# Writing one sum into another row, and tracing one block's routing later, in a fused attention, gated FFN and mixture-of-experts kernel

## The chip, the cores and the metric

One core of a Trainium2 chip runs the whole program. The metric is the device time of one execution in microseconds (us); lower is better.

## The reference, cut to what matters

```python
attn_out = _attn_ref(q, k, v)             # 4 x 8 heads x 576 positions x 64, window 128
x = attn_out -> [2304, 512]
gate = 1 / (1 + exp(-(x @ w_gate)));  val = x @ w_val          # 512 -> 1536
x = (gate * val) @ w_out                                        # 1536 -> 512
logits = xn @ en.T / tau; expert_idx = argmax(logits)           # 8 experts, one per token
out[mask] = gate_w * (relu(x[mask] @ w1[e]) @ w2[e])            # 512 -> 1024 -> 512
```

Everything is float32 to the outside. The kernel splits each matmul operand into a high and a low part and adds three products.

## The kernel before, in words

**Attention** comes first, then **the gated FFN's first matrix pair** (`w_gate`, `w_val`) in two passes over the 12 feature tiles f, each pass on two token chunks of 512. Both passes use a scheme of seven products instead of eight (`seven`): per f the products m5, m6, m7, m4 and m3 of f and m1 and m2 of f+1 alternate on TensorE (PE), six matmuls of 128x512 each. Their sums are collected on ScalarE (ACT; copies `c11`, `r1`, `c22`, the tanh `c21`) and VectorE (DVE). Line 438 is the matmul in `product`; L527, L532, L535, L538 and L542 are the ACT steps e1, e2, e6, e7 and e4; L531, L539 and L549 are the DVE additions.

In the second pass the gated values are not stored plainly. `keep_g` computes (gate+1)*val (L458), for each pair kk of feature tiles f = 2kk and 2kk+1 and both token halves, and stores through `put` (L461, a DMA issued by GpSimd, POOL) the four quarters A11, A12, A21, A22 and four sums S1 to S4 of them (L464 on DVE), because **the second matrix `w_out`** is applied to these 1024 tokens by a seven-product scheme again. In the even tile the values go to the halves `low` and `high` of a tile `gq`; in the odd tile they go to the gate's own row. The odd tile's second call (half 0) computes A12 into the gate's row (tile `c11`, in the profile `c`), issues its store, and then computes S4 = A12 - S2 into that same row and stores it. S4 occurs six times, once for each odd f. Rows are 128x512 tiles from a pool of ten.

While f runs, ACT and DVE also convert one tile of `w_out` (`split_wo`: L125 on ACT, L131, L132 and L134 on DVE into `cvwo`, then the cast `wo<-cvwo` at L105 on ACT and the subtraction at L121 on DVE), and POOL stores `cvwo`.

**The second matrix**: blocks of 256 tokens. Blocks 4, 3, 2, 1, 0 (`ROWS`) are done plainly (`mm2`, L914, 12 k-tiles in order); ahead of block 2 stands the scheme `strassen` for the 1024 tokens kept in the second pass (blocks 5 to 8): seven operands j, each two halves z (`mm3(j, z)`, L1228, 18 matmuls), with `ev3` scaling the results. The operand of j+1 is cast and subtracted at the head of step j (`split_op`, `oh` on ACT and `ol` on DVE). `prepare(0)` also builds four differences of `w_out` for each of six pairs (`split_w2`: `tq`, `th`, `tl`).

**Routing of a block**: `route_x` scales the two result banks into rows `xr` (L927) and squares them back into the banks (L928). `route_a` transposes `xr` (L954), copies to `xT` (DVE, L955), multiplies by the expert embeddings (`part`, L961), copies `parts` (ACT, L965), folds (`lp`, L969), normalises, takes the maximum and the exponentials, and stores the rows (two DMAs on POOL, L990). `route_b` counts ranks (`rk`, L1007 to L1012) and scatters token numbers (two indirect DMAs on POOL, L1030). Block 4 is routed during block 3's `mm2`; block 3 (`ROWS[1]`) is routed inside `strassen`: before the change in step j = 0.

PSUM banks: tag `m` has three, `s` two, `t` two, `o` one. The two banks of a block's `mm2`, the `a` accumulators and the `c` accumulator of half 0 share `m`; `part`, `lp` and the `c` accumulator of half 1 (first used in `mm3(1, 1)`) share `s`.

**What sets the order.** In the attention blocks and the first pass the order is written by hand. From the second pass on, a planner of the framework sets each engine's order at compile time, with its own estimate of durations; among instructions that are ready by the estimate, the one traced earlier goes first. On the chip each engine then runs its own list in that order, and waits where an estimate was off.

Of the kernel before, what the change touches and what calls it, by code (L numbers as in the profile page):

```python
# [15 lines left out]
ALU = mybir.AluOpType  # L16
# [25 lines left out]
ROWS = [4, 3, 2, 1, 0]  # L42
# [18 lines left out]
def attn_ffn_moe(ctx: ExitStack, tc: tile.TileContext, qkd, vd, wgv, w_out, emb, tau, w1, w2, cst, ids, out):  # L61
# [19 lines left out]
    def pt(tag, name, bufs):  # L81
        return ps.tile([P, 512], F32, tag=tag, name=name, bufs=bufs)

    def row(name):
        return mid.tile([P, DM + 16], F32, tag="r", name=name)[:, 0:DM + 1]

    def slot(shape, dt, name):
        return bpool.tile(shape, dt, tag="b", name=name)
# [359 lines left out]
    def g7_rows(name, kk, n=1):  # L448
        r = (NAMES.index(name) * KF // 2 + kk) * P
        return g7_d[r:r + n * P, :]  # L450

    def keep_g(f, half, gate, val):
        kk, odd = divmod(f, 2)
        if not odd and kk not in gq:
            gq[kk] = slot([P, 2, 512], F32, f"gq{kk}")
        low, high = gq[kk][:, 0, :], gq[kk][:, 1, :]
        o = gate if odd else (low, high)[half]
        nc.vector.scalar_tensor_tensor(out=o, in0=gate, scalar=1.0, in1=val, op0=ALU.add, op1=ALU.mult)  # L458

        def put(name, t):  # L460
            nc.gpsimd.dma_start(g7_rows(name, kk), t)  # L461

        def sums(name, t, x, y, op):
            nc.vector.tensor_tensor(out=t, in0=x, in1=y, op=op)  # L464
            put(name, t)

        if odd or not half:
            put(f"A{half + 1}{odd + 1}", o)
        if not odd and not half:
            sums("S3", high, high, low, ALU.subtract)  # L470
        elif odd and half:
            sums("S2", high, o, high, ALU.add)
            sums("S1", low, high, low, ALU.add)
        elif odd:
            sums("S4", o, o, high, ALU.subtract)

    def piece(mm, ev):
        def both():
# [243 lines left out]
    with tc.manual_schedule(engines={ENG.PE, ENG.DVE, ENG.Activation, ENG.Pool}):  # L722
        for i in range(NA, NU):
# [5 lines left out]
            late = unit_b(i)  # L729
# [87 lines left out]
    for f in range(KF):  # L817
        s, t = sv[f], sv[f + 1] if f + 1 < KF else None
# [127 lines left out]
    def route_a(b, ss, xr, c=None):  # L946
        nu = len(xr)
        lg = sm.tile([P, nu, E], F32, tag="lg", name=f"lg{b}")
        if c is None:
            xT = slot([P, nu, DM], F32, f"xT{b}")  # L950
        for u, x in enumerate(xr if c is None else []):
            q = pt("t", f"tl{b}_{u}", 2)
            for k in range(KD):
                nc.tensor.transpose(q[:, k * P:(k + 1) * P], x[:, k * P:(k + 1) * P], ident)  # L954
            nc.vector.tensor_copy(xT[:, u, :], q)  # L955
        part = pt("s", f"part{b}", 2)
        w = P // KD
        t0 = (2 * b * P - 256) % 512
        for k in range(KD):
            o = part[k * w:(k + 1) * w, 0:nu * P]  # L960
            nc.tensor.matmul(o.rearrange("p (u t) -> p u t", u=nu) if c is None else o, enT[:, k, :],  # L961
                             xT[:, :, k * P:(k + 1) * P] if c is None else c[k // 2][:, k % 2, t0:t0 + 2 * P],
                             start=True, stop=True, tile_position=(0, k * w))
        parts = row(f"parts{b}")[:, 0:nu * P]
        nc.scalar.copy(parts, part[:, 0:nu * P])  # L965
        lp = pt("s", f"lp{b}", 2)
        lps = [lp[:, u * E:(u + 1) * E] for u in range(nu)]
        for u in range(nu):
            nc.tensor.matmul(lps[u], parts[:, u * P:(u + 1) * P], fold, start=(u == 0), stop=(u == nu - 1),  # L969
                             skip_group_check=True)  # L970
        rn = rnorm(ss, nu, f"x{b}")
        mx = sm.tile([P, nu, 8], F32, tag="mx8", name=f"mx8{b}")
        ix = sm.tile([P, nu, 8], U32, tag="ix8", name=f"ix8{b}")
        nmx = sm.tile([P, nu], F32, tag="nmx", name=f"nmx{b}")
        sx = sm.tile([P, nu], F32, tag="sx", name=f"sx{b}")
        ex = sm.tile([P, nu, E], F32, tag="ex", name=f"ex{b}")
        for u in range(nu):
            nc.vector.tensor_scalar(out=lg[:, u, :], in0=lps[u], scalar1=rn[:, u:u + 1], scalar2=itau,
                                    op0=ALU.mult, op1=ALU.mult)
            nc.vector.max(out=mx[:, u, :], in_=lg[:, u, :])  # L980
            nc.vector.max_index(out=ix[:, u, :], in_max=mx[:, u, :], in_values=lg[:, u, :])
        nc.vector.tensor_scalar_mul(nmx, mx[:, :, 0], -1.0)
        for u in range(nu):
            nc.scalar.activation(out=ex[:, u, :], in_=lg[:, u, :], func=AF.Exp, bias=nmx[:, u:u + 1],
                                 accum_out=sx[:, u:u + 1])
        nc.vector.tensor_scalar_add(sx, sx, 1e-9)
        for u in range(nu):
            nc.vector.reciprocal(out=xr[u][:, DM:DM + 1], in_=sx[:, u:u + 1])
            t0 = (2 * b + u) * P
            (nc.sync if b == ROWS[-1] else nc.gpsimd).dma_start(x2_d[t0:t0 + P, :], xr[u])  # L990
        ixf = sm.tile([P, nu], F32, tag="ixf", name=f"ixf{b}")
        nc.vector.tensor_copy(ixf, ix[:, :, 0])
        oh = sm.tile([P, nu, E], BF16, tag="oh", name=f"oh{b}")
        for u in range(nu):
            nc.vector.tensor_scalar(out=oh[:, u, :], in0=iota8, scalar1=ixf[:, u:u + 1], scalar2=None,
                                    op0=ALU.is_equal)
        routed[b] = (oh, ixf)
# [221 lines left out]
    def mm3(j, z, k0=0, k1=KF // 2):  # L1219
        name, w, b = STEPS2[j]  # L1220
        first = j in (0, 1, 6)
        if first and k0 == 0:
            bk[b, z] = pt("s" if (b, z) == ("c", 1) else "m", f"{b}{z}_2", 2 if (b, z) == ("c", 1) else 3)
        for kk in range(k0, k1):
            wh, wl = w2_of(w, kk, z)
            xl, xh = (t[:, kk % 2, :] for t in g7[j][kk // 2])
            for y, (p, q) in enumerate(((wh, xh), (wl, xh), (wh, xl))):
                nc.tensor.matmul(bk[b, z], p, q, start=(first and kk == 0 and y == 0), stop=(kk == KF // 2 - 1 and y == 2),  # L1228
                                 skip_group_check=True)

    def ev3(j, z):
        def half(key, b):
            if key not in cq:
                cq[key] = slot([P, 2, 512], F32, f"c{key}")
            nc.scalar.mul(cq[key][:, z, :], bk[b, z], 0.5)

        def add(key, b):
            o = cq[key][:, z, :]
            nc.vector.scalar_tensor_tensor(out=o, in0=bk[b, z], scalar=0.5, in1=o, op0=ALU.mult, op1=ALU.add)

        if j == 0:
            half("11", "a")
        elif j == 2:
            half("12", "a")
        elif j == 3:
            half("22", "a")
            add("22", "c")
        elif j == 4:
            half("21", "a")
        elif j == 5:  # L1250
            add("12", "c")
        elif j == 6:
            add("11", "b")

    def strassen(late):
        xs2 = {}

        def rx(b):
            xs2[b] = route_xs(b, [cq["21"], cq["22"]] if b < 7 else [cq["11"], cq["12"]])

        def ra(b):
            route_a(b, *xs2.pop(b))

        load_op(2)
        mm3(0, 0, 0, 2)
        route_a(ROWS[1], *late)
        mm3(0, 0, 2)
        ev3(0, 0)
        mm3(0, 1, 0, 3)
        route_b(ROWS[1])  # L1270
        mm3(0, 1, 3)
        ev3(0, 1)
        for j in range(1, 7):
            split_op(j + 1)
            load_op(j + 2)
            if j == 5:
                load_g(ROWS[2])
            for z in range(2):
                mm3(j, z, 0, 3)
                for t in {(5, 0): [lambda: rx(5)], (5, 1): [lambda: ra(5)], (6, 0): [lambda: ra(6), lambda: route_b(5)],  # L1280
                          (6, 1): [lambda: route_b(6)]}.get((j, z), []):
                    t()
                mm3(j, z, 3)
                ev3(j, z)
                if (j, z) == (5, 1):
                    rx(6)
        split_g(ROWS[2])
        load_g(ROWS[3])
        return {0: [lambda: rx(7)], 1: [lambda: rx(8), lambda: ra(7)], 2: [lambda: route_b(7), lambda: ra(8)],
                3: [lambda: route_b(8)]}  # L1290
# [13 lines left out]
    for i, b in enumerate(ROWS):  # L1304
        inner = {}
        if i == STRASSEN_AT:
            inner = strassen(late)
# [29 lines left out]
        late = route_x(b, m)  # L1337
# [218 lines left out]
```

## Time and profile before

| what | value |
|---|---|
| time, median of 2 runs | 842.18 us (841.26 and 843.11) |
| the profiled execution | 838.87 us, span 837.1 us |
| PE busy | 796.3 us, 95% of the span |
| DVE busy | 567.8 us, 68% |
| ACT busy | 449.0 us, 54% |
| POOL busy | 208.2 us, 25% |
| mean granted TensorE clock | 0.98 |

The profile is of one execution. Times of rows are in us from the span's start. "Busy" is the time in which at least one instruction of the engine ran; "idle before" is the wait of an engine before an instruction, with what released it. A row of the time line reads: start, duration, engine, line, operation, out<-in, form, count, and in brackets the idle time before it. The second pass of `seven` runs from about 270 to 395 us, `mm2` of blocks 4 and 3 from 396 to 438 us, step j = 0 of the scheme from 438 to 458 us, steps j = 1 and 2 until about 476 us.

### The profile page before, as it was taken

Reading aid. Unit: us, or ns where it says so; the run is one execution under the profiler, and the core shown is the slowest. Engines: PE = TensorE matmul, PEld = TensorE weight load, DVE = VectorE, ACT = ScalarE, POOL = GpSimd, SP = SyncE. Lnnn points to the kernel's source line nnn. Section 1 sums busy time; section 2 is a strip of 40 time slices with the busy share of each in tenths; the row PEclk is TensorE's granted clock in tenths of the full one; section 3 lists DMA queues with packets and bytes.
Section 4 is the critical chain, followed back from the end, with each engine's and each line's share of the span. In section 5 each row is a group of like instructions: output and inputs, shape, how many; then the busy total and the mean of one; then the engine's idle time right before and its main releaser. Section 6 shows DMA issues by size and latency. Waiting matters only on the chain. (4 is left out here: it accounts for less than half of the span.)

```text
span 837.1 us, 15636 instructions
## 1 busy us (share of the span) xinstructions
PE 796.3 (95%) x5562; PEld 659.4 (79%) x5563; DVE 567.8 (68%) x1430; ACT 449.0 (54%) x946; POOL 208.2 (25%) x330
## 2 busy tenths in 40 slices
PE   8989999999999999896897999998999999999997
PEld 6767878878888887775685888776989989889796
DVE  7988977787799777766577666754846464455621
ACT  6888766666555544454446567744335443344510
POOL 6757422222000122222201203331231220310300
PEclk9999999999999999999797999999999999999999
DMA  8686567645754899878734684241568545545200
GB/s 276 190 272 213 193 240 226 244 168 214 245 221 154 327 332 323 297 270 301 246 106 142 182 278 175 102 141 49 165 183 330 182 160 188 179 152 177 80 23 17
DMA packets 71070, 166.61 MB, mean 199 GB/s; under 512 B 9511, under 2 KB 23591, under 8 KB 70992
## 3 DMA queue, kind: packets, MB, share of 16 engines
q1 hardware_dynamic: 61136, 136.08, 48.1%
q0 software_dynamic: 9856, 29.53, 9.8%
q8 instruction: 44, 0.72, 0.3%
q14 instruction: 34, 0.28, 0.1%
HBM read 116.20 MB, written 50.03 MB: 199 GB/s over the span
## 5 line engine op out<-in xcount | busy, mean ns | idle before, releaser
L1116 PE MATMUL h<-xe,weh 128*128 128x256 f32 (+4 forms) x512 | 107.7, 304 | 0.0
L1134 PE MATMUL z<-weh,h 128*128 128x512 f32 (+3 forms) x320 | 101.5, 396 | 0.9 <-DVE h L1119 0.6
L117 POOL TENSOR_SCALAR p<-p,rs 128x192 f32<-128x192 f32 x140 | 76.0, 560 | 102.1 <-DVE rs L268 51.7
L1116 PEld LDWEIGHTS h<-xe,weh 128*128 128x128 f32 x512 | 85.9, 194 | 1.2 <-DVE h L1119 0.2
L121 DVE TENSOR_TENSOR wel<-wer,weh 128x1024 fp32r<-128x1024 f32 x64 | 77.1, 1221 | 14.1 <-ACT weh L105 6.6
L914 PE MATMUL y<-wo,gh 128*128 128x512 f32 x240 | 80.0, 407 | 1.4 <-ACT gh L105 1.4
L1116 PE MATMUL h<-xe,wel 128*128 128x256 f32 (+4 forms) x256 | 77.7, 304 | 0.0
L252 ACT ACTIVATE p<-p,mx 128x192 f32<-128x192 f32 x144 | 64.0, 447 | 24.3 <-DVE mx L249 24.0
L105 ACT CAST weh<-wer 128x1024 fp32r<-128x1024 f32 x64 | 66.4, 1048 | 11.7 <-PE z L1134 9.7
L1118 ACT ACTIVATE h<-h 128x256 fp32r<-128x256 f32 (+4 forms) x64 | 26.7, 418 | 81.3 <-PE h L1116 76.5
L1134 PEld LDWEIGHTS z<-weh,h 128*128 128x128 f32 (+3 forms) x320 | 56.6, 181 | 15.6 <-DVE h L1119 1.0
L1139 POOL DMA_INDIRECT out<-y,cols x19 | 22.2, 1170 | 169.7 <-DVE y L1138 159.1
L1134 PE MATMUL z<-wel,h 128*128 128x512 f32 (+3 forms) x160 | 62.7, 392 | 0.0
L1119 DVE SCALAR_TENSOR_TENSOR h<-h,h 128x256 fp32r<-128x256 f32 (+4 forms) x64 | 29.5, 464 | 47.1 <-ACT h L1118 46.8
L914 PEld LDWEIGHTS y<-wo,gh 128*128 128x128 f32 x240 | 46.1, 194 | 12.5 <-ACT gh L105 1.8
L914 PE MATMUL y<-wo,gl 128*128 128x512 f32 x120 | 48.3, 403 | 4.6 <-DVE gl L121 4.6
L1138 DVE TENSOR_SCALAR y<-z,xg 128x512 f32<-128x512 f32 (+3 forms) x22 | 16.4, 747 | 49.3 <-PE z L1134 45.6
L1116 PEld LDWEIGHTS h<-xe,wel 128*128 128x128 f32 x256 | 49.7, 194 | 0.0
L461 POOL DMA_DIRECT2D g_d<-gq x24 | 13.3, 554 | 98.2 <-DVE gq L458 89.1
L249 DVE CUSTOM_DVE_ANT_0 p<-s,bias 128x192 f32<-128x192 f32 x96 | 30.7, 350 | 8.4 <-PE s L238 8.4
L238 PE MATMUL s<-qk 64*64 64x128 f32 (+2 forms) x864 | 34.2, 276 | 1.6 <-DVE mx L249 0.7
L281 PE MATMUL t<-cs,p 128*128 128x128 f32 x216 | 31.7, 279 | 3.9 <-ACT xf L105 2.5
(469 smaller groups left out, 2111.8 us busy)
## 6 DMA issues: line engine op xcount, KB each, us to landing
wer<-in_w SPq DMA_DIRECT2D x64, 512.0 KB, 7.1
wr<-in_wgv SPq DMA_DIRECT2D x24, 512.0 KB, 4.9
qk<-in_qkd SPq DMA_DIRECT2D x36, 320.0 KB, 5.1
ol<-g_d SPq DMA_DIRECT2D x21, 512.0 KB, 7.1
gl<-gT_d SPq DMA_DIRECT2D x15, 512.0 KB, 4.0
v<-in_vd SPq DMA_DIRECT2D x36, 192.0 KB, 3.4
wor<-in_w_out SPq DMA_DIRECT2D x12, 512.0 KB, 5.0
g_d<-gq POOLq DMA_DIRECT2D x24, 256.0 KB, 4.9
```

Of the source, the lines that this page charges most:

```text
L105: nc.scalar.copy(o, i)
L117: nc.gpsimd.tensor_scalar(out=t, in0=t, scalar1=r, scalar2=0.0, op0=ALU.mult, op1=ALU.add)
L121: e.tensor_tensor(out=o, in0=i, in1=h.bitcast(F32), op=ALU.subtract)
L238: nc.tensor.matmul(ss[u][y * 64:(y + 1) * 64, j * WK + d:j * WK + d + n], q[halves[u], a:a + 64], k[halves[u], a + c0:a + c0 + n], start=T ...
L249: nc.vector.tensor_tensor_reduce(out=o, in0=ss[u][:, j * WK:(j + 1) * WK], in1=bias, scale=-0.125, scalar=3.0e38, op0=ALU.add, op1=ALU.min ...
L252: nc.scalar.activation(out=o, in_=o, func=AF.Exp, scale=-1.0, bias=mx[:, z:z + 1], accum_out=su[:, z:z + 1])
L281: nc.tensor.transpose(t[:, z * P:(z + 1) * P], pf[:, z * P:(z + 1) * P], ident)
L914: nc.tensor.matmul(m, g[:, k % 4, u * P:(u + 1) * P], w[:, k % 3, :], start=(k == 0 and z == 0), stop=(k == KF - 1 and z == 2))
L1116: nc.tensor.matmul(m[:, :n], w[:, fs], x[:, k, :], start=(cnt == 0), stop=(cnt == 3 * KD - 1))
L1118: nc.scalar.activation(out=hh, in_=m[:, :n], func=AF.Relu)
L1119: nc.vector.scalar_tensor_tensor(out=hl, in0=m[:, :n], scalar=0.0, in1=hh.bitcast(F32), op0=ALU.max, op1=ALU.subtract)
L1134: nc.tensor.matmul(m[0:w, :], h, ww[:, ds], start=(cnt == 0), stop=(cnt == 3 * KE - 1))
```

## The change

The fourth sum is written into the row of the value (`val`, tile `r1`) and stored from there; the gate's row, from which A12 is stored, is no longer written again. And `route_a` and `route_b` of block 3 are traced in step j = 1 of the scheme, after the first half (three of six k-pairs) of `mm3(1, 0)` and of `mm3(1, 1)`, and not in step j = 0.

```diff
         elif odd:
-            sums("S4", o, o, high, ALU.subtract)
+            sums("S4", val, o, high, ALU.subtract)
...
         load_op(2)
-        mm3(0, 0, 0, 2)
-        route_a(ROWS[1], *late)
-        mm3(0, 0, 2)
-        ev3(0, 0)
-        mm3(0, 1, 0, 3)
-        route_b(ROWS[1])
-        mm3(0, 1, 3)
-        ev3(0, 1)
+        for z in range(2):
+            mm3(0, z)
+            ev3(0, z)
         for j in range(1, 7):
             split_op(j + 1)
             load_op(j + 2)
...
             for z in range(2):
                 mm3(j, z, 0, 3)
-                for t in {(5, 0): [lambda: rx(5)], (5, 1): [lambda: ra(5)], (6, 0): [lambda: ra(6), lambda: route_b(5)],
+                for t in {(1, 0): [lambda: route_a(ROWS[1], *late)], (1, 1): [lambda: route_b(ROWS[1])],
+                          (5, 0): [lambda: rx(5)], (5, 1): [lambda: ra(5)], (6, 0): [lambda: ra(6), lambda: route_b(5)],
                           (6, 1): [lambda: route_b(6)]}.get((j, z), []):
```

## Rows read from the trace of the kernel before

**Rows 1.** The page: busy time, share of the span and instructions.

```profile
PE 796.3 (95%) x5562; PEld 659.4 (79%) x5563; DVE 567.8 (68%) x1430; ACT 449.0 (54%) x946; POOL 208.2 (25%) x330
```

**Rows 2.** Second pass: length, busy (count) by engine, PEclk, DMA share, GB/s.

```profile
270.00:395.00 125.00, 114.22 (x489) 91.24 (x487) 89.84 (x146) 60.87 (x99) 27.17 (x48) 0.99 0.87 309
```

**Rows 3.** PE's waits, 270 to 420: total us, times, longest.

```profile
PE a L438 <- ACT r L535: 5.1, 3, 2.4
PE a L438 <- ACT c L538: 4.0, 2, 2.8
```

**Rows 4.** Time line of PE, its waits in the second pass.

```profile
325.20 0.50 PE L438 MATMUL a<-xh_(1, 'A22')_3954,wh 128*128 128x512 f32 x1 [1.18 <-ACT c L538]
...
344.27 0.50 PE L438 MATMUL a<-xh_(1, 'S3')_3943,wh 128*128 128x512 f32 x1 [2.43 <-ACT r L535]
...
365.67 0.50 PE L438 MATMUL a<-xh_(1, 'S3')_3943,wh 128*128 128x512 f32 x1 [2.02 <-ACT r L535]
...
387.42 0.17 PE L1007 MATMUL rk<-acc,one 128*128 128x8 bf16 x1 [1.54 <-DVE enT L795]
...
391.89 0.50 PE L438 MATMUL a<-xh_(1, 'A22')_3954,wh 128*128 128x512 f32 x1 [2.84 <-ACT c L538]
```

**Rows 5.** Time line of ACT, around PE's second wait.

```profile
343.11 0.62 ACT L105 CAST wo<-cvwo 128x512 fp32r<-128x512 f32 x1 [4.54 <-DVE cvwo L134]
343.64 0.58 ACT L535 COPY r<-a 128x512 f32<-128x512 f32 x1
```

**Rows 6.** Time line of DVE ahead of it: A12, the next sum, S4, cvwo.

```profile
333.40 0.68 DVE L458 SCALAR_TENSOR_TENSOR c<-c,r 128x512 f32<-128x512 f32 x1
...
335.08 0.69 DVE L531 TENSOR_TENSOR c<-c,b 128x512 f32<-128x512 f32 x1
339.04 0.69 DVE L464 TENSOR_TENSOR c<-c,gq 128x512 f32<-128x512 f32 x1 [3.28 <-DMA g_d<-c]
...
342.39 0.69 DVE L134 SCALAR_TENSOR_TENSOR cvwo<-wor,cvwo 128x512 int32<-128x512 int32 x1
```

**Rows 7.** DVE's waits, 280 to 470.

```profile
DVE c L464 <- DMA g_d<-c: 21.3, 6, 5.1
```

**Rows 8.** The stores of line 461, issue to landing.

```profile
DMA to landing us min/median/max: 3.9/5.4/6.1
```

**Rows 9.** Stretches of the second pass, columns as in group 2.

```profile
276.00:286.00 10.00, 10.00 (x45) 8.18 (x44) 6.31 (x9) 3.85 (x7) 1.36 (x2) 1.00 0.98 389
...
345.60:366.60 21.00, 18.98 (x84) 15.40 (x83) 15.38 (x24) 9.92 (x16) 5.10 (x9) 1.00 0.85 294
366.60:370.00 3.40, 3.40 (x10) 2.57 (x9) 0.90 (x2) 1.53 (x2) 0.00 (x0) 0.53 0.80 276
```

**Rows 10.** Time line of DVE at the end of the second pass.

```profile
398.51 0.68 DVE L458 SCALAR_TENSOR_TENSOR c<-c,r 128x512 f32<-128x512 f32 x1
...
400.32 1.22 DVE L121 TENSOR_TENSOR gl<-gl,gh 128x1024 fp32r<-128x1024 f32 x1
```

**Rows 11.** Time line of PE at the start of block 4.

```profile
401.59 0.79 PE L914 MATMUL y<-wo,gl 128*128 128x512 f32 x1 [4.57 <-DVE gl L121]
```

**Rows 12.** Time line of PE in step 0 of the scheme.

```profile
446.78 1.08 PE L961 MATMUL part<-xT,enT 128*32 128x256 f32 x8 [4.81 <-DVE xT L955]
...
449.23 1.09 PE L954 MATMUL tl<-cs,xr 128*128 128x128 f32 x4
450.40 1.22 PE L1228 MATMUL a<-oh,wo 128*128 128x512 f32 x2
...
451.85 1.05 PE L954 MATMUL tl<-cs,xr 128*128 128x128 f32 x4
```

**Rows 13.** Time line of ACT there: block 3's square, its `parts`.

```profile
449.62 0.61 ACT L928 ACTIVATE y<-xr 128x512 f32<-128x512 f32 x1
...
457.18 0.37 ACT L965 COPY parts<-part 128x256 f32<-128x256 f32 x1 [2.08 <-PE part L961]
```

**Rows 14.** Time line of DVE after block 3's routing.

```profile
463.25 5.77 DVE L121 TENSOR_TENSOR ol<-ol,oh 128x1024 fp32r<-128x1024 f32 x5 [0.17 <-ACT oh L105]
```

**Rows 15.** Two later stretches, columns as in group 2.

```profile
391.90:407.40 15.50, 9.56 (x28) 7.02 (x29) 10.06 (x17) 5.78 (x8) 6.36 (x12) 0.68 0.98 358
...
446.80:455.40 8.60, 8.02 (x33) 5.59 (x34) 7.20 (x30) 7.08 (x15) 0.00 (x0) 0.50 0.19 64
```

## The prediction

> **What bounds the kernel now.** I read the page first. PE is busy for 95% of the span, DVE for 68% [rows 1], so a change pays only where it takes away idle time of PE or a stretch at the lower clock. Next I cut the span into stages. In the second pass PE is busy for 114.22 of 125.00 us [rows 2], so 10.8 us are idle in the stage that the first edit touches. The list of PE's waits puts 9.1 us of that down to ACT's copies out of the `a` bank [rows 3]; the time line gives the five large waits, 1.18, 2.43, 2.02, 1.54 and 2.84 us, together 10.01 us [rows 4].
>
> Why is ACT late? I follow the second wait back. ACT copies `r1` at 343.64, but only because the cast of `w_out` ahead of it on its list had waited 4.54 us for DVE's `cvwo` [rows 5]. DVE delivers `cvwo` at 342.39 + 0.69 = 343.08, six places behind S4 on its list. S4 had stood 3.28 us waiting for a DMA, the store of A12, which reads the row that S4 writes; A12 itself was ready at 333.40 + 0.68 = 334.08 [rows 6]. There are six such waits, one for each odd f, 21.3 us in total and up to 5.1 [rows 7]. So the chain is: store of A12, S4, `cvwo`, cast on ACT, copy out of `a`, PE. DVE's own idle time is cheap where PE is not behind it: of 21.3 us only about half reaches PE.
>
> **The S4 edit, term by term.** It removes no instruction and adds none. S4 reads A12 and the half `high` and writes `r1`, whose only reader by then, the product that made A12, stands earlier on the same engine. So it needs no DMA.
>
> (a) The first three waits of PE have six matmuls of another product ahead of them, so a copy of 0.58 us [rows 5] fits under that. They go entirely: 1.18 + 2.43 + 2.02 = 5.63 us [rows 4].
>
> (b) The last two belong to f = 11. No next f fills in, so PE waits for the copy out of `a` each time: 0.58 us [rows 5] and about 0.1 us for the signal, say 0.7. What goes is 1.54 - 0.7 + 2.84 - 0.7 = 3.0 us [rows 4]. The embedding copy that releases the first of these also stands behind an S4 (waiting up to 5.1 us [rows 7]).
>
> (c) After the third wait PE runs for 3.40 us at a granted clock of 0.53, thus mostly at 1.2 GHz [rows 9]. That work takes 3.40 x 0.53 = 1.8 us at 2.4 GHz, so 1.6 us come back if the clock fell because of the wait. A wait of 2.43 us shortly before did not have that effect (345.6 to 366.6 is at 1.00), so the bounds are 0 and 1.6; I take 1.6, since the slow stretch begins within 1 us of the end of that wait.
>
> (d) The cost. S4 will no longer be ranked behind what fills its wait in the plan; it comes directly after A12 and pushes the additions behind it back by 0.69 us. Six times this falls into gaps of DVE (15.38 busy of 21.00 us, [rows 9]). Once it doesn't: at f = 11, A12 starts at 398.51 and the `gl` subtraction, for which PE waits 4.57 us, comes after it [rows 10, 11]. I charge 0.6 us there. Bounds 0 and 0.69.
>
> Row `r1` is now held until S4's store lands (5.4 us at the median, [rows 8]) and `c11` is let go that much earlier, one row for one: nothing. On POOL's queue the S4 stores only move earlier, and nothing waits behind them that is late.
>
> Sum of the edit: -5.63 - 3.0 - 1.6 + 0.6 = -9.6 us. Bounds: 0, if another wait takes over, and 21.3, all that S4 waits for, on top of which there is nothing.
>
> What is late next? DMA has to carry the same bytes in less time: 294 GB/s over 21.00 us is 6.2 MB, and without the 2.02 us of waiting that is 325 GB/s; the stage has run at 389 with PE unstalled [rows 9]. So it fits, but with a DMA share that was 0.85 already. DVE at 15.38 of 19.0 us is at 81%.
>
> The page "DMA: Bandwidth & Descriptors" of the Trainium skill, section "Anatomy of one DMA", puts such a transfer at 2.0 us plus its bytes at 436 GB/s, an estimate of 2.6 us for 256 KB. By that S4 would wait for only 21.3 - 6 x 2.8 = 4.5 us and PE would get little back. The trace does not agree: it shows 5.4 us at the median, under a busy DMA, so the 9.6 stands.
>
> **The routing edit.** Moved, of block 3: in `route_a` eight transposes, two `xT` copies, eight `part` matmuls, the `parts` copy, four `lp` matmuls, the normalisation and maxima on DVE, ACT's root and exponentials, two row stores on POOL; in `route_b` the rank matmuls, DVE's short integer steps and two scatters on POOL. On POOL they go past nothing, since no other work is traced there in steps 0 and 1; on SP nothing of them stands. Nobody reads block 3's rows or ranks before several blocks later. The slot for `xT` is now asked for after `oh` of step 2 and `ol` of step 3.
>
> What it cannot do is take away the largest wait in this place. PE stands for 4.81 us before a `part` matmul at 446.78, and then runs 8.6 us at 0.50 [rows 12, 15]. That looks like the moved routing, but block 3's square is still running at 449.62 [rows 13], and its transposes come at 449.23 and 451.85 [rows 12]: the `part` at 446.78 is block 4's, whose `xT` copy stands behind `split_w2` on DVE. The edit does not touch it.
>
> The same instructions run on PE before and after. Gain, at most: if the transposes leave the slow stretch, about half of 1.09 + 1.05 us [rows 12]; but matmuls of the scheme then run there instead, so nearer 0. Loss: `mm3(0, 1)` needs the bank that the square frees at 449.62 + 0.61 = 450.23 [rows 13]. Before, the transposes of 449.23 fill the time until then; if they now come later, PE idles for 1.0 us. Since a planner takes what is ready, they may well stay. I take +0.5 us, between -1.0 and +1.0.
>
> **Sum.** -9.6 + 0.5 = -9.1 us. The profiled execution took 838.87 us, 3.3 under the median of 842.18; against it the sum gives 829.8, against the median 833.1. Forecast: 833 us.
>
> **Rivals.**
> 1. *Hidden or replaced.* The S4 waits go, but PE waits as long for something else: DMA (share 0.85 to 0.98, [rows 9]) brings weights late, or ACT's list has another such cast. For: half of DVE's waits never reached PE. Against: every one of the five waits of PE follows an S4, and PE runs the stretch from 276 to 286 without a break at 389 GB/s [rows 9]. Also here: the planner orders S4 behind a store anyway, so that the edit does nothing. Gain 0 to 4 us: 838 to 843, say 841.
> 2. *More than the stage.* The planner, with new times, also orders block 4's `xT` copy ahead of `split_w2`: 4.81 us, and 8.6 x 0.50 = 4.3 us of clock [rows 12, 15], or part of that; or the clock holds at the start of block 4, where it is 0.68 over 15.5 us [rows 15]. For: small wins of time change ties in a plan. Against: nothing in either edit moves that copy. 833 - 9 = 824.
> 3. *Slower.* Place: between `mm3(1, 0)` and `mm3(1, 1)`. The second needs one of the two `s` banks, and `part` and `lp` of block 3 now ask for both just ahead of it. From the second transposes to the end of `parts` it took 457.18 + 0.37 - 451.85 = 5.7 us [rows 12, 13]; half of `mm3(1, 0)`, nine matmuls at 114.22/489 = 0.23 us [rows 2], covers 2.1. The wait is 3.6 us, and if DVE has its five operand subtractions of 5.77 us [rows 14] ahead of the `xT` copies, 9.4. With the clock behind it as behind `part`, 4.3 us [rows 15], that is 13.7 against the 9.6 gained: 842 + 4 = 846. It ends slower only if wait and clock together pass 9.6 us, thus not without DVE's queue. Against: a bank that is free goes to the accumulator if the planner places it first.
>
> **Chances.** Forecast 0.60 (828 to 837), rival 1 0.17, rival 2 0.12, rival 3 0.11. The range 825 to 841 takes in the forecast with its bounds, most of rival 1 and half of rival 2; about 0.2 is left out. This kernel's measurement tells about 2% (17 us) from no change: faster than 825 needs nearly all of rival 2, 0.09; slower than 859 needs more than rival 3, 0.03; within 0.88.
>
> **What would show it.** After: no wait of an L464 `r<-c,gq` for a DMA; PE's waits on `a` in the second pass at about 1.4 us, against 9.1; the pass about 10 us shorter; the wait at `part` in step 0 still there, with its slow stretch; block 3's `part` in step 1 without a wait. Wrong if DMA shares reach 1 there with PE waiting for weights, if PE waits at the head of `mm3(1, 1)`, or if `part` of block 4 no longer waits.

## The result and the profile after

The changed kernel took **830.12 us** (median of 2 runs, 829.94 and 830.30), against 842.18 for the kernel before: a ratio of 0.986, with a 95% interval of 0.981 to 0.990. The profiled execution took 829.94 us, 8.93 under that of before, where the sum of the prediction had said 9.1. The forecast of 833 us was that sum taken off the median of before, 842.18, which rests on two runs; in the experiments below the kernel before has medians of 838.4 to 840.2 us, and it is the 829.8 us counted from the profiled execution that came true. By the bound of about 2% this is no change; by the intervals of this study it is a gain of about 1.2% (0.9885 with six runs, number 3).

The page of the kernel after, first its busy times, then the second pass in the columns of [rows 2]:

```profile
span 828.1 us, 15649 instructions
PE 794.4 (96%) x5562; PEld 657.1 (79%) x5563; DVE 568.7 (69%) x1430; ACT 449.1 (54%) x946; POOL 207.2 (25%) x330
```

```profile
270.00:385.00 115.00, 111.49 (x484) 89.03 (x483) 89.73 (x144) 59.95 (x96) 26.24 (x48) 1.00 0.93 331
```

The counts of each engine are those of [rows 1]: no work was added or removed. The second pass is where the difference is: PE idles for 3.5 us of 115.0, where it idled for 10.8 of 125.0 [rows 2], the clock is at 1.00, and the DMA share rose from 0.87 to 0.93.

Four of the waits of PE in the kernel after (what it waited for: total us, times, longest) answer to [rows 3], [rows 11] and [rows 12]:

```profile
PE a L438 <- ACT r L535: 2.8, 5, 0.7
PE a L438 <- ACT c L538: 0.7, 1, 0.7
PE y L914 <- DVE gl L121: 5.2, 1, 5.2
PE part L961 <- DVE xT L955: 4.2, 1, 4.2
```

9.1 us behind ACT have become 3.5, and none of these waits is above 0.72 us. The line with 4.2 us is the `part` matmul of block 4, which the prediction said the routing edit would not touch.

DVE's waits for stores, kernel after (the line that answers to [rows 7] has no counterpart, since no wait of an S4 is left):

```profile
DVE gq L464 <- DMA g_d<-gq: 5.6, 4, 2.0
```

And the same line in the kernel before, which the prediction did not price:

```profile
DVE gq L464 <- DMA g_d<-gq: 2.2, 2, 1.9
```

All of these are waits of S2. In the even tile S3 is written into `high` and stored from there, and in the odd tile S2 overwrites it (A11 is stored from `low`, and A21, which `high` held first, goes only into S3 and is not stored). The waits grew from 2.2 to 5.6 us, and not because DVE arrives earlier: the store takes longer. The issue of S3's store on POOL and the S2 that waits for it, for f = 4 and 5, before and after:

```profile
324.42 0.54 POOL L461 DMA_DIRECT2D g_d<-gq  x1
329.60 0.69 DVE L464 TENSOR_TENSOR gq<-c,gq 128x512 f32<-128x512 f32 x1 [0.33 <-DMA g_d<-gq]
```

```profile
321.28 0.54 POOL L461 DMA_DIRECT2D g_d<-gq  x1
329.67 0.69 DVE L464 TENSOR_TENSOR gq<-c,gq 128x512 f32<-128x512 f32 x1 [2.02 <-DMA g_d<-gq]
```

Counted from the end of the issue, DVE came to S2 after 4.3 us before and after 5.8 us now; the store released it after 4.6 us before and after 7.9 us now. Over all stores of line 461 the longest landing rose from 6.1 us [rows 8] to 8.4. Which transfers they wait behind is not shown.

The time line of PE in the kernel after, its waits from 330 us on, answers to [rows 4] and [rows 11]:

```profile
341.87 0.50 PE L438 MATMUL a<-xh_(1, 'S3')_3943,wh 128*128 128x512 f32 x1 [0.59 <-ACT r L535]
...
362.05 0.50 PE L438 MATMUL a<-xh_(1, 'S3')_3943,wh 128*128 128x512 f32 x1 [0.59 <-ACT r L535]
...
381.35 0.50 PE L438 MATMUL a<-xh_(1, 'S3')_3943,wh 128*128 128x512 f32 x1 [0.72 <-ACT r L535]
383.69 0.50 PE L438 MATMUL a<-xh_(1, 'A22')_3954,wh 128*128 128x512 f32 x1 [0.66 <-ACT c L538]
...
393.98 0.79 PE L914 MATMUL y<-wo,gl 128*128 128x512 f32 x1 [5.16 <-DVE gl L121]
```

**Where the time went**, followed by the same instruction in both traces. The last wait of the pass ends at 383.69 and ended at 391.89: 8.2 us earlier. The first `gl` matmul of block 4 starts at 393.98 and started at 401.59: 7.6 earlier, since the `gl` wait grew by 0.59. `part` of block 4 starts at 437.85 and started at 446.78: 8.9 earlier. The end of the span is 9.0 earlier (837.1 to 828.1). So the gain is complete ahead of the place to which the routing was moved, and nothing is added or lost from there on.

The step from 7.6 to 8.9 is the clock at the start of block 4 and a shorter wait at `part`. The ten microseconds from the first `gl` matmul on, first before, then after:

```profile
401.50:411.50 10.00, 9.91 (x31) 7.89 (x32) 4.20 (x6) 0.62 (x1) 2.16 (x4) 0.69 0.97 332
```

```profile
393.90:403.90 10.00, 9.93 (x34) 8.03 (x35) 3.49 (x5) 0.62 (x1) 2.16 (x4) 0.76 0.97 342
```

10.0 x (0.76 - 0.69) = 0.7 us came from the clock and 4.81 - 4.25 = 0.56 from the wait at `part`: 7.6 + 0.7 + 0.6 = 8.9. The two executions had come to the pass within 0.2 us of each other (its first wait for ACT ends at 271.52 before and at 271.73 after); among the profiles below these starts lie up to 2.2 us apart, so a difference of two spans there is no finer than that.

### The profile page after: what moved, and what is told of

Its sections match the earlier page's. It is cut to its first block, busy times and chain, and to the rows that moved or that the text cites. A ratio compares the mean times of both kernels' runs of the same rounds, so it can differ in the third digit from the quotient of the medians.

```text
span 828.1 us, 15649 instructions
## 1 busy us (share of the span) xinstructions
PE 794.4 (96%) x5562; PEld 657.1 (79%) x5563; DVE 568.7 (69%) x1430; ACT 449.1 (54%) x946; POOL 207.2 (25%) x330
## 5 line engine op out<-in xcount | busy, mean ns | idle before, releaser
L1030 POOL DMA_INDIRECT tab_d<-ids_sb,ai x18 | 22.3, 1237 | 98.3 <-DVE xr L988 60.7
```

The source lines that it names most:

```text
L1030: nc.gpsimd.indirect_dma_start(out=tab_d, out_offset=IOA(ap=ai[:, u:u + 1], axis=0), in_=ids_sb[:, t:t + 1], in_offset=None)
```

## The experiments

Each was run with the kernel before on the same chip, and its ratio is to that. Numbers 1, 2 and 4 shared one chip, numbers 5 to 8 a second, numbers 3 and 9 a third. "Span" is that of the one execution that was profiled.

**1. The S4 edit alone.**

```diff
-            sums("S4", o, o, high, ALU.subtract)
+            sums("S4", val, o, high, ALU.subtract)
```

> Only the S4 edit; block 3 is routed in step 0 as before. Theory (the S4 waits reach TensorE through ACT's cast of w_out): all of the gain is here, 8.5 to 9.5 us under the kernel before, ratio 0.989, and the five waits of the second pass fall from 10.0 to about 2.8 us. Rival (the gain is the routing's): within 2 us of before.

829.56 us, 0.988 (0.986 to 0.991); span 827.8 against 828.1 of the whole change.

**2. The routing edit alone** (the other hunk of the diff).

> Only the routing edit; S4 is written into the gate's row as before. Theory: within 1 us of the kernel before, and the wait at block 4's part stays at 4.8 us. Rival (the gain is the routing's): 6 to 9 us faster, with that wait gone or the stretch at the lower clock behind it shorter.

838.43 us, 0.999 (0.998 to 1.001). Its waits of PE and of DVE:

```profile
PE part L961 <- DVE xT L955: 4.8, 1, 4.8
PE a L438 <- ACT r L535: 4.6, 3, 2.6
...
PE a L438 <- ACT c L538: 3.5, 3, 2.8
```

```profile
DVE c L464 <- DMA g_d<-c: 20.3, 6, 5.0
```

The waits that the prediction gave to S4 are still there (8.1 us of PE behind ACT against 9.1, 20.3 us of DVE against 21.3), and the wait of block 4's `part` is still 4.8 us. The routing edit is worth nothing that these runs can measure (between 2.1 us won and 0.8 us lost, by the interval).

**3. Both once more, on one chip.** The whole change, and the S4 edit alone.

> The changed kernel itself, beside the S4 edit alone on the same chip. The theory (all of the gain comes from S4; at the routing's place the two traces differ by nothing that lasts): 829.5 to 830.5 us, within 1 us of the S4 edit alone, 9 to 10 us under the kernel before. Rival (the routing edit is worth something once the second pass is faster): 2 us or more below the S4 edit alone, or above it.

> The S4 edit alone once more, on the same chip as the whole change. Theory: 829 to 830.5 us, no different from the whole change within 1 us. Rival: the routing edit gives or costs 2 us or more, so this one ends that far on the other side.

830.55 us, 0.989 (0.987 to 0.991), and 830.19 us, 0.988 (0.986 to 0.990). The two differ by 0.4 us and their intervals overlap almost wholly: nor is the routing worth anything on top of S4.

**4. S4 into the value's row for the first three odd tiles only, and for the last three only.**

```diff
-            sums("S4", val, o, high, ALU.subtract)
+            sums("S4", val if kk < 3 else o, o, high, ALU.subtract)
```

> Before, with S4 in the value's row for f = 1, 3, 5 alone. If each S4 wait acts on TensorE by itself and at its place, this brings the waits of 1.18 and 2.43 us less the 0.3 and 0.6 that stayed in the changed kernel: about 2.7 us. If time won early is lost again at the later S4 waits (an engine that arrives earlier just waits longer there), 0 to 1 us.

```diff
-            sums("S4", val, o, high, ALU.subtract)
+            sums("S4", val if kk >= 3 else o, o, high, ALU.subtract)
```

> Before, with S4 in the value's row for f = 7, 9, 11 alone. If the waits act each at its place: 2.02 - 0.6, the 1.6 us of lower clock, 3.0 at f = 11, less 0.6 at the start of block 4, plus what follows from these: 5.5 to 6.5 us, and with the early half the sum of the whole edit. If the waits are not independent: 8 us or more, as the whole edit.

The first half: 838.13 us (832.4 to 842.1 in 12 runs), 0.998 (0.996 to 1.000). The last half: 832.22 us, 0.992 (0.990 to 0.995). By their ratios of 0.24% and 0.77% of 839.57 they are worth 2.0 and 6.5 us, together 8.5 against the 9.8 of both at once, a difference that the intervals do not settle. The halves are not alike: the time line of PE with the first half done:

```profile
342.75 0.50 PE L438 MATMUL a<-xh_(1, 'S3')_3943,wh 128*128 128x512 f32 x1 [0.62 <-ACT r L535]
365.36 0.50 PE L438 MATMUL a<-xh_(1, 'S3')_3943,wh 128*128 128x512 f32 x1 [3.14 <-ACT r L535]
...
391.45 0.79 PE L438 MATMUL a<-xh_(1, 'A22')_3954,wh 128*128 128x512 f32 x1 [2.84 <-ACT c L538]
```

Its stretches behind the last two waits:

```profile
365.36:369.50 4.14, 4.14 (x12) 3.27 (x13) 1.83 (x3) 1.97 (x3) 0.25 (x1) 0.66 0.91 282
...
391.50:396.00 4.50, 4.50 (x11) 3.53 (x12) 1.69 (x5) 1.59 (x3) 0.13 (x1) 0.50 0.97 319
```

The early waits fell to 0.46 and 0.62, but the next S4 that still waits for its store holds PE for 3.14 us, where it was 2.02 [rows 4]: part of the time won early was waited for again there. Another part went to S2, which waited 1.51, 1.89 and 2.11 us for the stores of S3, where the kernel before has 1.86, 0.33 and none: those stores landed later here too (7.2 to 8.0 us after the issue). This execution had come to the pass 1.0 us later than that of before (272.51 against 271.52) and ends the last wait of the pass 0.4 us earlier, so it won 1.4 us in the pass; the clock fell behind that wait, and the span is 837.1, as before. The 2.0 us of the 12 runs (0.3 to 3.6 by the interval) stand between the two values expected, 2.7 and 0 to 1, and decide for neither. With the last half done the early waits stay, 1.49 and 2.83, with the clock at 1.00 behind the second, and the three late ones are gone or at their natural size. The 6.5 us are those expected if each wait acts at its place. So a wait that a store sets was worth its length here only where no later wait of the same kind took it back.

**5. Block 4's `xT` ahead of the differences of `w_out`** (on top of the change): five of the six `split_w2` are traced one block later.

```diff
-            for kk in range(6):
+            for kk in range(1):
                 split_w2(kk)
...
         elif i == 1:
+            for kk in range(1, 6):
+                split_w2(kk)
             split_op(1)
```

> The changed kernel, with five of the six split_w2 of prepare(0) traced in prepare(1), so that block 4's copies to xT come ahead of them on VectorE. Theory (the wait of 4.2 us at part is block 4's, behind split_w2, and the lower clock follows from it): that wait is gone, and 4 to 8 us of the changed kernel with it: 822 to 826, ratio to the kernel before 0.979 to 0.984. Rival (VectorE is full there, and the wait only moves to step 1 of the scheme, which needs the last differences of w_out): 828 to 831, ratio 0.987 to 0.990, with a wait of 3 to 5 us at a matmul of step 1. Rival (the wait is block 3's): still at part, 4 us.

826.46 us, 0.985 (0.983 to 0.988); span 824.6, thus 3.5 under the kernel after (2.7 by the two ratios to the kernel before, 0.985 and the 0.989 of number 3), less than the 4 to 8 expected. From the last wait of the pass on, this execution is 5.4 us shorter (385.58 to 824.6 against 383.69 to 828.1); it had come there 1.9 us later, after a clock of 0.93 between 50 and 100 us. Its time line of PE no longer has a wait at `part`, and two at the head of step 1:

```profile
443.11 0.50 PE L1228 MATMUL c<-oh,th 128*128 128x512 f32 x1 [1.14 <-ACT oh L105]
444.55 0.54 PE L1228 MATMUL c<-ol,th 128*128 128x512 f32 x1 [0.72 <-DVE ol L121]
```

PE then ran from 443 to 452 us at a clock of 0.81. That the wait at `part` is gone shows that the 4.81 us of [rows 12] were block 4's copy behind `split_w2` on DVE, as the prediction said, and that the routing of block 3 had no part in them.

**6. Block 4's gated operand loaded and split during the pass** (on top of the change).

```diff
+        if f == KF - 1:
+            load_g(ROWS[0])
+            split_g(ROWS[0])
...
-    load_g(ROWS[0])
...
-    split_g(ROWS[0])
```

> The changed kernel, with the split of block 4's first operand traced in the last tile of the second pass, after its m5, and not behind the pass. Theory (the two waits of 1.4 and 5.2 us at the start of block 4 are latency of VectorE's list, and the stretch at 0.72 clock follows from them): they shrink to under 2 us, and 5 to 8 us come off the changed kernel: 822 to 825, ratio 0.979 to 0.983. Rival (time won there is given back at part, 9 us longer waiting): 829 to 831, ratio 0.988 to 0.990.

831.11 us, 0.990 (0.988 to 0.993): nothing won against the change. The waits of 1.38 and 5.16 us at the start of block 4 are gone, and PE waits further on, 9.9 us where it was 1.38 + 5.16 + 4.25 = 10.8:

```profile
408.52 1.22 PE L915 MATMUL y<-wo,gh 128*128 128x512 f32 x2 [2.55 <-ACT gh L105]
...
439.68 1.08 PE L962 MATMUL part<-xT,enT 128*32 128x256 f32 x8 [7.35 <-DVE xT L956]
```

The expected 5 to 8 us did not come; its rival, that the time is given back at `part`, did. `part` starts 54.5 us behind the last wait of the pass, and 54.2 in the kernel after: DVE's row of work up to the `xT` copy sets this end, whether PE stands ahead of it or behind it.

**7. S3 into the value's row too** (on top of the change): no row that a store still reads is written any more.

```diff
-            sums("S3", high, high, low, ALU.subtract)
+            sums("S3", val, high, low, ALU.subtract)
+            s3_row[kk] = val
...
-            sums("S2", high, o, high, ALU.add)
+            sums("S2", high, o, s3_row.pop(kk), ALU.add)
```

> The changed kernel, with S3 written into the value's row too, so that S2 and S3 wait for no store of gq (5.6 us of VectorE's waits in the changed kernel). Theory (the waits of 0.3 to 0.6 us that stayed in TensorE's second pass come from VectorE's waits for gq, by cvwo and the cast, as the S4 waits did): they go, 1 to 1.5 us off the changed kernel: ratio 0.9865. Rival (they come from the order of the cast and the copy on ScalarE's list alone): no change, ratio 0.988 to 0.989, the waits still there.

827.20 us, 0.986 (0.984 to 0.989); span 826.1, 2.0 under the kernel after. Its waits of PE on `a`:

```profile
PE a L438 <- ACT r L536: 1.4, 2, 0.7
...
PE a L438 <- ACT c L539: 0.7, 1, 0.7
```

The three waits of 0.26, 0.59 and 0.59 us that the kernel after still had are gone, and so are DVE's waits for `gq` stores. Their cause was the store of S3 in `high`: S2 still goes there, but nothing is stored from it any more.

**8. Numbers 5, 6 and 7 together, with block 3's operand split a block earlier as well.**

```diff
+    split_g(ROWS[1])
...
-        if i + 1 < NB2 and i + 1 != STRASSEN_AT:
+        if i and i + 1 < NB2 and i + 1 != STRASSEN_AT:
```

> All of these together (xT early, block 4's operand early, S3 in the value's row), and block 3's operand split ahead of block 4's matmuls as well. If the gains stand apart: 812 to 818, ratio 0.967 to 0.975. If VectorE's list between the second pass and step 1 is what bounds the stretch: 822 to 826, ratio 0.979 to 0.984.

**820.29 us**, 0.978 (0.975 to 0.980): the fastest version of this study, ahead of both kernels. Its span is 9.1 us under that of the kernel after, more than the 3.5 and 2.0 of numbers 5 and 7; the other 3.6 (4.6 by the ratios) come from number 6, worth nothing alone, and block 3's operand together, which were not separated. Neither expectation was met: the time lies between the 812 to 818 us of gains that stand apart and the 822 to 826 us of a stretch bound by DVE's list. PE's largest wait now:

```profile
437.47 0.80 PE L1231 MATMUL c<-oh,th 128*128 128x512 f32 x1 [7.48 <-ACT oh L105]
```

**9. The operand of step 1 split after the second pair of `split_w2`** (on top of number 8).

```diff
             for kk in range(1, 6):
                 split_w2(kk)
-            split_op(1)
+                if kk == 1:
+                    split_op(1)
```

> The combined version (S3 and S4 in the value's row, block 4's operand early, most of split_w2 later), with the operand of step 1 split after the second pair of split_w2 and not behind the sixth. There PE waited 7.48 us at step 1 for the cast oh. Theory A (the wait is a matter of order: oh only stands behind five th casts): the wait nearly goes and the clock holds, 6 to 9 us less, about 812 to 815. Theory B (split_w2 is a chain of DVE and ACT taking turns, 3.8 us for each pair, and step 1 needs all six pairs): the wait only spreads over several smaller ones for th and tl, 0 to 3 us less, 817 to 821.

821.42 us, 0.977 (0.975 to 0.980): the same as number 8. The waits of PE:

```profile
PE c L1231 <- ACT th L105: 4.6, 3, 1.8
PE c L1231 <- DVE tl L121: 1.7, 3, 0.8
```

One wait of 7.5 us has become six of 6.3 us in sum. It was not the order on ACT: `split_w2` is a chain in which DVE and ACT wait for each other, and step 1 needs its end.

## Why the prediction was right, and where a term was off

**The forecast case happened.** S4 was late by its own store, and the chain store, S4, `cvwo`, cast, copy out of `a`, PE was the right one: with the S4 edit alone the time is all there (number 1), without it DVE's wait for the store of A12 is there in full (number 2). Term by term:

(a) *The first three waits go entirely, 5.63 us*: too large. They fell to 0.26, 0.59 and 0.59 us, so 1.18 + 2.43 + 2.02 - 1.44 = 4.2 went. Its sign, PE's waits on `a` at about 1.4 us, did not come true: they are 3.5, these 1.44, the 1.38 of (b) and 0.68 at 271.73, a wait that the kernel before has too. The prediction looked at S4's store only, and of the DMA it asked whether the same bytes fit, not whether each store lands as fast. The same chain has a second store ahead of it, that of S3, as ACT and DVE of the kernel after show (start, duration; idle time before in brackets):

```profile
340.00 0.68 DVE L134 SCALAR_TENSOR_TENSOR cvwo<-wor,cvwo 128x512 int32<-128x512 int32 x1
```

```profile
340.72 0.62 ACT L105 CAST wo<-cvwo 128x512 fp32r<-128x512 f32 x1 [2.00 <-DVE cvwo L134]
341.24 0.58 ACT L535 COPY r<-a 128x512 f32<-128x512 f32 x1
```

The cast still waits 2.00 us for `cvwo` where it waited 4.54 [rows 5]. What holds DVE there now is S2, which waits for the store of S3 in `high` (2.02 us at 329.67): number 7 takes away just these waits, and the three go.

(b) *The last two shrink to 0.7 each, 3.0 us*: right. They are 0.72 and 0.66 us: 1.54 + 2.84 - 1.38 = 3.0. The copy and its signal were priced from one row and were the natural size, which also stays in number 7.

(c) *The lower clock, 1.6 us*: right in kind, large in size. There is no slow stretch in the pass any more:

```profile
345.60:362.00 16.40, 15.86 (x69) 12.50 (x68) 13.03 (x22) 7.70 (x14) 4.57 (x9) 1.00 0.96 327
362.00:386.70 24.70, 23.28 (x101) 18.12 (x101) 18.33 (x37) 14.38 (x24) 5.71 (x11) 1.00 0.92 326
```

But what PE was busy for up to the last wait fell by 1.0 us only. First before, then after:

```profile
270.00:391.89 121.89, 111.21 (x477) 89.07 (x475) 88.28 (x143) 59.46 (x96) 26.98 (x48) 0.99 0.87 309
```

```profile
270.00:383.69 113.69, 110.18 (x479) 87.94 (x477) 89.07 (x144) 59.95 (x96) 26.24 (x48) 1.00 0.94 333
```

The two rows give the whole account of the pass: idle time 121.89 - 111.21 = 10.68 against 113.69 - 110.18 = 3.51, that is 7.2 us, and 1.0 us of busy time: 8.2, where (a), (b) and (c) made 10.2. (The 0.2 us by which the execution after came later to the pass are in this; without them the busy time fell by 1.2.)

(d) *0.6 us at the start of block 4*: right. S4 now stands between A12 and the `gl` subtraction, on DVE of the kernel after:

```profile
390.30 0.68 DVE L458 SCALAR_TENSOR_TENSOR c<-c,r 128x512 f32<-128x512 f32 x1
...
391.50 0.68 DVE L464 TENSOR_TENSOR r<-c,gq 128x512 f32<-128x512 f32 x1
392.71 1.21 DVE L121 TENSOR_TENSOR gl<-gl,gh 128x1024 fp32r<-128x1024 f32 x1
```

The wait grew from 4.57 to 5.16 us, by 0.59.

**The routing, +0.5 us**: the medians of number 3 differ by 0.4 us and those of number 2 by 1.1, which these runs can't tell from nothing. The first transposes of block 3 stayed where they had filled PE's time, ahead of the second half of step 0; only what follows moved, in the kernel after:

```profile
440.29 1.09 PE L954 MATMUL tl<-cs,xr 128*128 128x128 f32 x4
441.47 1.22 PE L1228 MATMUL a<-oh,wo 128*128 128x512 f32 x2
...
450.32 0.60 PE L954 MATMUL tl<-cs,xr 128*128 128x128 f32 x4
455.11 0.64 PE L961 MATMUL part<-xT,enT 128*32 128x256 f32 x8
...
457.31 0.49 PE L1228 MATMUL c<-oh,th 128*128 128x512 f32 x1
```

So the loss that the prediction feared (1.0 us of idle PE if they came later) did not come.

**The sum came out in part by luck**, since its errors cancel. Terms (a) and (c) were 1.4 and 0.6 us too large, and the routing 0.5 us too dear. What the prediction had left out was worth 1.3 us: 0.7 of clock at the start of block 4 and 0.56 at `part`. That clock was named, as part of rival 2, but not counted. -10.2 + 2.0 + 0.6 - 1.3 = -8.9 us.

**The rivals.** Rival 1 (hidden or replaced) was not the case at S4 as a whole: no load appears among PE's waits in the pass. But it is what happened to 1.4 us of (a), and to part of the time of the first three S4 in number 4, through stores that land later and not through late weights. Rival 2 (more than the stage): its lever was real but the change did not pull it. Its 4.81 us and the clock behind stayed (4.25 us; 0.51 against 0.50 [rows 15]):

```profile
437.90:446.50 8.60, 8.02 (x31) 5.25 (x32) 6.68 (x30) 7.01 (x15) 0.20 (x1) 0.51 0.51 162
```

Number 5 pulls it, and gets 5.4 us at this place and not 9, since step 1 then waits 1.14 and 0.72 us for its operand and runs its first 9 us at a clock of 0.81 (1.7 us). Rival 3 (a wait for an `s` bank ahead of `mm3(1, 1)`) did not appear: the matmul at 457.31, its first, has no idle time before it, and neither has block 3's `part` at 455.11. The delay that it named is in the order all the same: before, `mm3(1, 1)` follows `mm3(1, 0)` and step 2 comes behind both; now 14 matmuls of step 2 (from 452.87 on) stand between them and fill, with `part` and `lp`, the 4.5 us.

**The DMA time.** The stores of gate-row tiles take 5.5 us to land at the median in the kernel after, with a DMA share of 0.93 in the pass. The rule of the Trainium skill's page "DMA: Bandwidth & Descriptors", section "Anatomy of one DMA", from which the prediction estimated 2.6 us for them, is again not what this trace shows; and the gain, which by that rule would have been small, follows the measured time.

## What to carry to other kernels

A sum that overwrites a tile whose store is still under way made its engine stand until the store landed (2.4 to 5.1 us, six times here), and with it everything behind it on that engine's list; look for the row that nobody reads any more and write there. Before pricing the removal of such a wait, list every other wait of the same kind on the same chain (here S2 behind the store of S3) and allow for stores that land later once the stage is shorter: the waits of S2 grew from 2.2 to 5.6 us although DVE came to them later after the issue than before. A wait moved away from one place pays only if the end of that engine's chain moves too: an early operand was worth nothing by itself (number 6); that it is worth something once the copies behind it come earlier as well is likely from number 8, but was not separated there.

## What was not expected of the hardware

The clock did not answer to the length of a wait alone. In the kernel before it stayed at 1.00 behind a wait of 2.43 us and fell behind one of 2.02 [rows 4, 9]; with the routing edit alone it fell behind the first (2.57 us), and with the last three S4 edited it stayed at 1.00 behind 2.83 us. Behind the last wait of the pass, 2.84 us in both, it was 1.00 in the kernel before and 0.50 with the first three S4 edited. The rows behind the 2.57 us, the 2.83 us and the last wait of the kernel before:

```profile
346.00:349.00 3.00, 3.00 (x9) 2.40 (x8) 0.69 (x1) 1.53 (x2) 0.00 (x0) 0.54 0.75 234
```

```profile
344.65:349.00 4.35, 4.35 (x19) 3.60 (x20) 3.11 (x5) 2.52 (x4) 0.25 (x1) 1.00 0.83 275
```

```profile
391.90:396.30 4.40, 3.02 (x13) 2.18 (x13) 2.86 (x6) 2.65 (x4) 0.88 (x3) 1.00 0.97 330
```

With the first three S4 edited it is the row of 391.50 under number 4. One profiled execution of each kernel was read, so what decides it is left open. The slow stretches of these rows cost from 3.40 x 0.47 = 1.6 us [rows 9] to 4.50 x 0.50 = 2.3 us, and others nothing: that is the uncertainty to give to such a term.
